# Attention followed by a gated feed-forward: reordered loads, and the mask-product scoring for the second half too

## The chip, the cores and the metric

The kernel runs on one core of one Trainium2 chip. The metric is the device time of one execution in microseconds; the time before is the median of six runs. A profile is one further execution with the hardware profiler on; its "span" runs from the first to the last recorded instruction.

## What is computed

Attention with 4 batches, 8 heads, 768 positions and head dimension 64, restricted to a window, and then a feed-forward with a relu gate. Cut to what matters:

```python
scores = scale * np.matmul(q, k.transpose(0, 1, 3, 2))
is_global = pos[None, :] < n_global                      # 8 global keys
is_local = (rel >= 0) & (rel < n_local)                  # the last 96 keys
keep = is_global | is_local
dist = np.where(is_global & ~is_local, n_local, np.abs(rel))
scores = np.where(keep, scores - slopes[h] * dist, -1e9) # a slope for each head
a = softmax(scores)
x = (a @ v) with heads joined                            # [3072, 512]
out = (np.maximum(x @ w_gate, 0) * (x @ w_val)) @ w_out  # 512 -> 1536 -> 512
```

Inputs and output are in float32; the kernel multiplies in bfloat16.

## The kernel before

The work is cut into eight *halves*, each half of the 768 positions of one batch (384 rows, all eight heads). Half 0 and half 1 belong to batch 0. A half goes through these steps, each a small function that is called from a hand-written order:

- `load_qk`, `load_v_half`: q and k come by SyncE's (SP) DMA queue into two staging buffers `qs`, `ks`; v comes by GpSimd's (POOL) queue, cast to bfloat16 on the way, into `vbuf`. The weights come by POOL's queue too, in three groups of four column blocks for the gate (`wg[0..2]`, `load_gate`) and for the value matrix (`wv[0..2]`, `load_val`), and as one piece for the output matrix (`wo_sb`).
- `piece_cast(s, p)`: casts q and k of head pair p to bfloat16.
- `piece_t(s, p)`: six TensorE transpositions into one PSUM bank, and copies from there into `qTb` and into the key tiles `kT` (`put_keys`).
- Scores, in one of two ways. For halves 0 and 1, `piece_bias` writes the distance bias into PSUM with a matmul (`sid` x `dd`), and `piece_score` adds q x k onto it, with one head in the upper and one in the lower 64 rows; an Exp on ScalarE (ACT) gives the weights `es`. The column groups of this way are in `first_groups`. For the later halves, `piece_qk` multiplies both heads of a pair at once, using a `qTb` in which each head's other 64 rows are zero; ACT takes the Exp, and VectorE (DVE) multiplies it with `m_all`, the exponentials of the bias, which `mask(h)` makes on ACT, one for each of the eight heads.
- Weights times v: `piece_av_wide` for halves 0 and 1 (a product with ones for the denominators, a product with v, then Ln, Exp and a multiplication into `xT`), `piece_av` for the later ones.
- `ffn_pieces(c)`: for each of twelve column blocks a gate product of four matmuls of 128x384 (relu on ACT, or on DVE for the blocks in `by_vector`) and a value product of four (multiplied by the relu on DVE into `ht`); and then six output pieces. In the list `f1`, item 2 fc is the gate product of block fc and item 2 fc + 1 is its value product.

From half 1 on the attention of the next half is woven between the feed-forward pieces of the one before. The order is written out by hand in every engine's program order (`manual_schedule`); `weave` places attention pieces at given fractions of the feed-forward work. The feed-forward has two PSUM banks in the stage around the change (`ffps2`), and `grelu` four buffers.

In the stage of the change POOL's program order is: value group 0 (behind a one-element copy that waits for half 0's `xT`), casts of half 1, v of half 1, gate group 1, a cast, fills of `kT` and `vbuf`, value group 1, fills of `qTb[0]`, gate group 2, fills of ones, value group 2. The q and k of half 1 are loaded from the middle of half 0's attention on (`load_qk_after(1, nc.vector, True)`, whose small memset stands on DVE and holds SP's DMAs back). PE's order is the first four gate products of half 0, half 1's attention with eight further products of half 0 in it, four more, then `other_pools()`; half 0's last eight products come in the second weave:

```python
    weave(f1_1[0 : 4 * GW],
          [(0.1 * h, lambda h=h: mask(h)) for h in range(H)],
          [(0.62 + 0.12 * p, lambda p=p: piece_t(2, p)) for p in range(HP)])
    weave(f1_0[G[2]] + f1_1[G[2]] + f2_0 + f2_1,
          spread(attention_pieces(2), 0.2, 0.9), ...
```

## Time and profile before

| | before |
|---|---|
| median of six runs | 254.24 us (252.97 to 256.0) |
| the profiled execution's own time | 254.06 us |
| its span | 252.3 us |
| TensorE busy | 241.5 us, 96% of the span |
| VectorE, ScalarE, GpSimd busy | 131.7, 157.5, 89.8 us |
| DMA | 33.15 MB in 77704 packets |
| granted TensorE clock | 1.00 |

The span and the execution's own time differ by 1.8 us, which lies around the recorded instructions. The page divides the span into 40 equal slices of 6.3 us; each digit is the busy share of an engine in tenths. "PE" is TensorE's matmuls, and their ends are modelled, so a busy PE is not a PE at its peak. The chain of waits is followed back from the last instruction: at each step to what released it, or to the instruction before it on the same engine. A group's row gives line, engine, operation, tiles and shapes, count, then total and mean time, then the engine's idle time just before and what ended it.

### The profile page before, as it was taken

How to read it: one execution, taken by the hardware profiler on the slowest of the kernel's cores; microseconds unless marked ns; L12 is line 12 of the kernel's file. 1: busy time of each engine (PE TensorE's matmuls, PEld its weight loads, DVE VectorE, ACT ScalarE, POOL GpSimd, SP SyncE). 2: the span in 40 equal slices, each digit the busy share in tenths (PEclk: the TensorE clock that was granted, in tenths of full speed). 3: DMA queues.
4: the chain of work that ended last, by engine and by line, in shares of the span. 5: the costliest groups of instructions: out<-in, count | busy, mean ns of one | idle time of the engine just before them, and what ended most of it. 6: DMA issues, size and time to landing. Idle time of an engine off the chain costs nothing.

```text
span 252.3 us, 4928 instructions
## 1 busy us (share of the span) xinstructions
PE 241.5 (96%) x1763; PEld 144.2 (57%) x1763; DVE 131.7 (52%) x338; ACT 157.5 (62%) x318; POOL 89.8 (36%) x214
## 2 busy tenths in 40 slices
PE   7788898999999999999999999999999999999994
PEld 3556565665555566556665566556565566556643
DVE  3635364695555557616662567617762557524410
ACT  5787555736676687657785687657785687553312
POOL 7818994600377426801537066302530000000000
PEclk9999999999999999999999999999999999999999
DMA  6999999980899983969376967729441200020012
GB/s 183 157 266 186 158 188 250 197 141 5 247 167 235 175 244 73 146 108 285 73 123 71 233 183 165 47 86 290 93 99 42 83 3 1 0 97 31 0 44 83
DMA packets 77704, 33.15 MB, mean 131 GB/s; under 512 B 53488, under 2 KB 74736, under 8 KB 77680
## 3 DMA queue, kind: packets, MB, share of 16 engines
q1 hardware_dynamic: 45824, 24.93, 36.3%
q0 software_dynamic: 31856, 7.91, 32.2%
q8 instruction: 14, 0.23, 0.4%
q14 instruction: 10, 0.08, 0.1%
...
## 4 chain that ended last, share of the span: by engine, by line
PE 80%; DMA 6%; DVE 5%; ACT 4%; SPq 2%; issue 1%; POOL 0%; ACTq 0%; DVEq 0%
PE ff_ps L521 24%; PE ff_ps L500 23%; PE ff_ps L487 21%; DMA qs<-in_q_dram 5%; PE av_ps L399 5%; PE qk_ps L371 4%; DVE xT L416 2%; SPq L131 2%; DVE ht L502 1%; ACT grelu L493 1%; PE av_ps L283 1%; ACT rcp L413 1%; ACT lnd L408 1%; DMA out_dram<-osb 1%; PE av_ps L433 1%
## 5 line engine op out<-in xcount | busy, mean ns | idle before, releaser
L500 PE MATMUL ff_ps<-xT,wv 128*128 128x384 bf16 x384 | 78.1, 326 | 1.5 <-ACT grelu L493 0.6
L487 PE MATMUL ff_ps<-xT,wg 128*128 128x384 bf16 x384 | 77.7, 326 | 0.3 <-DMA wg<-in_moe_w_gate_dram 0.3
L493 ACT ACTIVATE grelu<-ff_ps 128x384 bf16<-128x384 f32 x94 | 46.0, 490 | 32.7 <-PE ff_ps L487 18.4
L502 DVE TENSOR_TENSOR ht<-ff_ps,grelu 128x384 bf16<-128x384 f32 x96 | 53.2, 555 | 25.0 <-PE ff_ps L500 19.8
L521 PE MATMUL ff_ps<-wo_sb,ht 128*128 128x512 bf16 x276 | 64.5, 379 | 0.0
L416 DVE TENSOR_TENSOR xT<-av_ps,rcp 64x384 bf16<-64x384 f32 x48 | 26.6, 555 | 44.8 <-ACT rcp L413 44.1
L500 PEld LDWEIGHTS <-wv 128*128 128x128 bf16 x384 | 36.0, 97 | 24.5 <-issue 3.4
L487 PEld LDWEIGHTS <-wg 128*128 128x128 bf16 x384 | 36.1, 97 | 23.7 <-DMA wg<-in_moe_w_gate_dram 0.8
L383 DVE TENSOR_TENSOR es<-es,m_all 128x432 bf16<-128x432 bf16 (+5 forms) x108 | 33.2, 336 | 22.6 <-ACT es L374 22.1
L374 ACT ACTIVATE es<-qk_ps 128x432 bf16<-128x432 f32 (+2 forms) x72 | 37.9, 528 | 10.1 <-PE qk_ps L371 8.2
L521 PEld LDWEIGHTS <-ht 128*128 128x128 bf16 x276 | 25.8, 97 | 26.8
L296 POOL CAST kc<-ks 128x384 bf16<-128x384 f32 x20 | 9.7, 530 | 61.2 <-DMA ks<-in_k_dram 61.2
L408 ACT ACTIVATE lnd<-av_ps 64x384 f32<-64x384 f32 x48 | 23.3, 485 | 11.6 <-PE av_ps L399 11.0
L526 ACT COPY osb<-ff_ps 128x512 f32<-128x512 f32 x23 | 13.5, 586 | 23.3 <-PE ff_ps L521 22.5
L371 PE MATMUL qk_ps<-qT,kT 128*128 128x432 bf16 (+5 forms) x108 | 24.8, 286 | 0.0
L155 POOL DMA_DIRECT2D vbuf<-in_v_dram x28 | 24.4, 877 | 0.6 <-issue 0.6
L399 PEld LDWEIGHTS <-vbuf 128*128 128x128 bf16 x216 | 18.0, 98 | 7.4
L399 PE MATMUL av_ps<-es,vbuf 128*128 128x216 bf16 (+4 forms) x216 | 21.0, 226 | 0.0
L371 PEld LDWEIGHTS <-kT 128*128 128x128 bf16 x108 | 10.6, 98 | 7.6
L358 ACT ACTIVATE es<-qk_ps 128x864 bf16<-128x864 f32 (+3 forms) x16 | 10.5, 708 | 5.1 <-PE qk_ps L353 5.1
L304 POOL CAST qz<-qs 128x192 bf16<-128x192 f32 x40 | 12.7, 373 | 2.3 <-DMA qs<-in_q_dram 1.9
L413 ACT ACTIVATE rcp<-lnd 128x384 f32<-128x384 f32 x24 | 12.5, 522 | 0.8
...
## 6 DMA issues: line engine op xcount, KB each, us to landing
out_dram<-osb SPq DMA_DIRECT2D x23, 256.0 KB
...
```

What stands on the lines that cost most here:

```text
L155: nc.gpsimd.dma_start(out=v_dst(b, NG + r0, NG + r0 + n, j), in_=v[b, :, KT * j + r0 : KT * j + r0 + n, :].rearrange("h p d -> p h d"))
L371: nc.tensor.matmul(ps[:, c : c + n_], lhsT=kt[:, j, :], rhs=qd[:, :, :, a : a + w], start=True, stop=True)
L374: nc.scalar.activation(es[:, 0:cols], ps[:, 0:cols], AF.Exp, bias=0.0, scale=scale)
L383: nc.vector.tensor_mul(e4, e4, mk)
L399: nc.tensor.matmul(av3[:, :, a : a + w], lhsT=vb[:, j, z0 : z0 + 128], rhs=es[:, c : c + NN * w].rearrange("k (n p) -> k n p", n=NN), star ...
L408: nc.scalar.activation(ln[o0 : o0 + 64], av[d0 : d0 + 64, 0:QH], AF.Ln, bias=0.0, scale=1.0)
L416: nc.vector.tensor_tensor(xT_of[s][r, p, :], av_of[s, p, e_][r, 0:QH], rc[r], op=ALU.mult)
L487: nc.tensor.matmul(psg[:, 0:QH], lhsT=w_of(wg, dc, fc), rhs=xT[:, dc, :], start=(dc == 0), stop=(dc == N_DC - 1))
L493: nc.scalar.activation(gr, psg[:, 0:QH], AF.Relu, bias=0.0, scale=1.0)
L500: nc.tensor.matmul(psv[:, 0:QH], lhsT=w_of(wv, dc, fc), rhs=xT[:, dc, :], start=(dc == 0), stop=(dc == N_DC - 1))
L502: nc.vector.tensor_tensor(ht[:, fc, :], psv[:, 0:QH], st[fc], op=ALU.mult)
L521: nc.tensor.matmul(ps2, lhsT=ht[:, fc, n * 128 : (n + 1) * 128], rhs=wo_sb[:, fc, :], start=(fc == 0), stop=(fc == N_FC - 1))
```

## The change

Loads: the q and k of half 1 are no longer loaded during half 0's attention. Value group 0 is issued as soon as the fourth v piece of half 0 has landed, then gate group 1 behind gate group 0 and value group 1 behind value group 0, each held back by a one-element copy on POOL (`hold`) from the earlier landing's bytes. The q and k of half 1 follow behind gate group 1 (`load_qk_behind`), its v behind the first k, gate group 2 behind POOL's cast of pair 3, value group 2 behind half 1's first v piece, and half 2's q and k behind gate group 2.

Scoring: half 1 is scored by `piece_qk`, so its bias matmuls go and its mask products come; `mask` runs for all heads on ACT directly behind the first four gate products, instead of in the first weave. The two head rows of `qTb[1]` are copied separately, on ACT, and POOL zeroes the other rows. Casts of half 1 stand on ACT (pair 0), DVE (1 and 2) and POOL (3).

Order: all 24 gate and value products of half 0 now come before or inside half 1's attention, so the second weave has eight items less and its fractions are set anew. Four warm-up matmuls behind half 0's attention go. The pool of `es` has four buffers instead of three, and in the stage of half 1 the score pool has four banks in four tiles instead of two tiles of two banks.

```diff
--- before.py
+++ after.py
@@ -60,8 +60,7 @@
     by = {(h_, j): (j, a, w, m) for h_, j, a, w, m in spans}
     banks_of_half[0] = [[by[0, 0]], [by[0, 1]], [by[0, 2], by[0, 3]]]
     banks_of_half[1] = [[by[1, 2], by[1, 5]], [by[1, 3], by[1, 6]], [by[1, 4]]]
-    first_groups = [[[by[0, 0], by[0, 1]], [by[0, 2], by[0, 3]]],
-                    [[by[1, 4], by[1, 3]], [by[1, 5], by[1, 2], by[1, 6]]]]
+    first_groups = [[[by[0, 0], by[0, 1]], [by[0, 2], by[0, 3]]]]
 
     const = ctx.enter_context(tc.tile_pool(name="const", bufs=1))
     setupp = ctx.enter_context(tc.tile_pool(name="setupp", bufs=1))
@@ -77,19 +76,19 @@
     P = {}
     first = ExitStack()
     second = ExitStack()
-    P["es"] = second.enter_context(tc.tile_pool(name="es2", bufs=4))
+    P["es"] = first.enter_context(tc.tile_pool(name="es2", bufs=4))
     P["qk"] = first.enter_context(tc.tile_pool(name="qkps2", bufs=3, space=bass.MemoryType.PSUM))
 
     def second_pools():
         first.close()
-        P["qk"] = second.enter_context(tc.tile_pool(name="qkps3", bufs=2, space=bass.MemoryType.PSUM,
+        P["es"] = ctx.enter_context(tc.tile_pool(name="es", bufs=4, reuse_waits="tile"))
+        P["qk"] = second.enter_context(tc.tile_pool(name="qkps3", bufs=4, space=bass.MemoryType.PSUM,
                                                     reuse_waits="tile"))
         P["ff"] = second.enter_context(tc.tile_pool(name="ffps2", bufs=2, space=bass.MemoryType.PSUM,
                                                     reuse_waits="tile"))
 
     def other_pools():
         second.close()
-        P["es"] = ctx.enter_context(tc.tile_pool(name="es", bufs=3, reuse_waits="tile"))
         P["qk"] = ctx.enter_context(tc.tile_pool(name="qkps", bufs=3, space=bass.MemoryType.PSUM,
                                                  reuse_waits="tile"))
         P["ff"] = ctx.enter_context(tc.tile_pool(name="ffps", bufs=3, space=bass.MemoryType.PSUM,
@@ -177,15 +176,26 @@
     def load_val(i):
         load_w(wv[i], moe_w_val, i * GW * 128, (i + 1) * GW * 128)
 
-    def load_qk_after(s, eng, by_pairs=False):
+    def hold(dst, src):
+
+        nc.gpsimd.tensor_copy(dst, src)
+
+    def load_qk_behind(s, src):
 
         qs_of[s] = stage.tile([128, H, NN * D], FP32, name="qs")
         ks_of[s] = stage.tile([128, H, NN * D], FP32, name="ks")
-        step = 2 if by_pairs else H
+        for t in (ks_of[s], qs_of[s]):
+            hold(t[0:1, 0:H:2, 0:1], src[0:1, 0, 0:HP].unsqueeze(2))
+        for p in range(HP):
+            load_qk(s, 2 * p, 2 * p + 2)
+
+    def load_qk_after(s, eng):
+
+        qs_of[s] = stage.tile([128, H, NN * D], FP32, name="qs")
+        ks_of[s] = stage.tile([128, H, NN * D], FP32, name="ks")
         for t in (qs_of[s], ks_of[s]):
-            eng.memset(t[0:1, 0:H:step, 0:1], 0.0)
-        for h in range(0, H, step):
-            load_qk(s, h, h + step)
+            eng.memset(t[0:1, 0:1, 0:1], 0.0)
+        load_qk(s, 0, H)
 
 
     for p in range(HP):
@@ -247,8 +257,8 @@
             copy = nc.gpsimd.tensor_copy
             if s == 0:
                 copy = (nc.vector.tensor_copy, nc.scalar.copy, nc.scalar.copy, nc.vector.tensor_copy)[p]
-            elif s == 1 and p == 1:
-                copy = nc.scalar.copy
+            elif s == 1 and p < 3:
+                copy = (nc.scalar.copy, nc.vector.tensor_copy, nc.vector.tensor_copy)[p]
             copy(
                 qk[:, i].rearrange("t n e d -> t e n d"),
                 src[:, 2 * p : 2 * p + 2, :].rearrange("t e (n d) -> t e n d", n=NN))
@@ -284,12 +294,12 @@
                                  lhsT=qk[:, i, n],
                                  rhs=ident, is_transpose=True,
                                  start=(i == 0 and n == 0), stop=(i == 1 and n == NN - 1))
-        if s < 2:
+        if s == 0:
             nc.vector.tensor_copy(qTb[s][:, p, 0, :], tp[:, 0, :])
         else:
             for e in range(2):
                 r = slice(64 * e, 64 * e + 64)
-                nc.vector.tensor_copy(qTb[s % 2][r, p, e, :], tp[r, 0, :])
+                (nc.scalar.copy if s == 1 else nc.vector.tensor_copy)(qTb[s % 2][r, p, e, :], tp[r, 0, :])
         put_keys(nc.vector.tensor_copy, nc.vector.tensor_copy, kt, tp[:, 1, :], half)
 
     def piece_cast_k(s, p):
@@ -418,8 +428,10 @@
 
     def piece_av_wide(s, p):
 
-        todo = [t for group in first_groups[s] for t in group]
-        if p % 2 == 1:
+        todo = [t for group in (first_groups[0], banks_of_half[1])[s] for t in group]
+        if p % 2 == 1 and s == 1:
+            av = [P["qk"].tile([128, 512], FP32, name="qk_ps") for _ in range(2)]
+        elif p % 2 == 1:
             t = P["qk"].tile([128, 2, 512], FP32, name="qk_ps")
             av = [t[:, i] for i in range(2)]
         else:
@@ -430,9 +442,10 @@
                 es, c = es_of[s, p, j]
                 for e in range(2):
                     z0 = D + 2 * D * (2 * p + e)
+                    x = es[:, e, c : c + NN * w] if s == 0 else es[:, c + e * NN * w : c + (e + 1) * NN * w]
                     nc.tensor.matmul(av3[64 * e : 64 * e + 64, :, a : a + w],
                                      lhsT=ones if what == 0 else vbuf[0][:, j, z0 : z0 + D],
-                                     rhs=es[:, e, c : c + NN * w].rearrange("k (n p) -> k n p", n=NN),
+                                     rhs=x.rearrange("k (n p) -> k n p", n=NN),
                                      start=(i == 0), stop=(i == len(todo) - 1),
                                      skip_group_check=True)
         ln = rc_pool.tile([128, QH], FP32, name="lnd")
@@ -455,17 +468,15 @@
             return (C(0) + X(lambda: load_v_globals(0), lambda: load_v(0, 0), lambda: load_v(0, 1),
                              lambda: load_v(0, 2), lambda: load_v(0, 3), lambda: load_gate(0))
                     + C(1) + T(0) + BI(0, 0, 1) + C(2) + T(1) + SC(0, 0, 1) + BI(1, 0) + SC(1, 0) + C(3) + T(2)
-                    + BI(1, 1) + SC(1, 1) + BI(2, 0) + T(3) + X(lambda: copy_v_globals(0, 1, 4), lambda: load_qk_after(1, nc.vector, True))
+                    + BI(1, 1) + SC(1, 1) + BI(2, 0) + T(3) + X(lambda: copy_v_globals(0, 1, 4))
                     + SC(2, 0) + BI(2, 1) + SC(2, 1)
                     + BI(3, 0) + SC(3, 0) + BI(3, 1) + SC(3, 1)
                     + AW(0) + AW(1) + AW(2)
-                    + AW(3) + X(second_pools, lambda: warm(4)))
+                    + AW(3) + X(second_pools))
         if s == 1:
             f = [[x] for x in fill]
-            return (T(0) + BI(0, 0, 1) + T(1) + SC(0, 0, 1) + T(2) + BI(1, 0) + SC(1, 0) + BI(1, 1) + SC(1, 1)
-                    + T(3) + BI(2, 0) + SC(2, 0) + BI(2, 1) + SC(2, 1) + f[0] + BI(3, 0) + SC(3, 0)
-                    + f[1] + BI(3, 1) + SC(3, 1) + f[2] + AW(0) + f[3] + AW(1) + f[4]
-                    + AW(2) + f[5] + f[6] + AW(3) + f[7])
+            return (f[0] + C(0) + C(1) + T(0) + C(2) + T(1) + f[1] + QK(0) + T(2) + QK(1) + T(3) + f[2] + QK(2) + f[3] + QK(3)
+                    + AW(0) + AW(1) + f[4] + AW(2) + f[5] + AW(3) + f[6] + f[7])
         AV = lambda p: [(0.29, lambda e=e: piece_av(s, p, e)) for e in range(2)]
         g = QK(3)
         a = AV(2)
@@ -562,44 +573,50 @@
     copy_v_globals(0, 4, NT)
     for p in range(HP):
         nc.gpsimd.memset(kT[0][p][:, 6, NG + 48 : 128].bitcast(mybir.dt.uint32), 0)
-
-    nc.gpsimd.tensor_copy(wv[0][0:1, 0, 0:1], xT_of[0][0:1, 0, 0:1])
+    hold(wv[0][32:33, 0, 0:1], v_dst(0, 32, 33, 3)[:, 0, 0:1])
     load_val(0)
-    piece_cast(1, 0)
-    load_v_half(1)
-    piece_cast(1, 2)
+    for e in range(2):
+        nc.gpsimd.memset(qTb[1][64 - 64 * e : 128 - 64 * e, :, e, :].bitcast(mybir.dt.uint32), 0)
+    hold(wg[1][0:1, 0, 0:1], wg[0][0:1, 0, 0:1])
     load_gate(1)
-    piece_cast(1, 3)
+    hold(wv[1][0:1, 0, 0:1], wv[0][0:1, 0, 0:1])
+    load_val(1)
+    load_qk_behind(1, wg[1])
     for p in range(HP):
         nc.gpsimd.memset(kT[1][p][:, 3, 32:128].bitcast(mybir.dt.uint32), 0)
         nc.gpsimd.memset(kT[1][p][:, 6, NG + 48 : 128].bitcast(mybir.dt.uint32), 0)
     nc.gpsimd.memset(vbuf[1][:, NT - 1, :].bitcast(mybir.dt.uint32), 0)
-    load_val(1)
+    hold(v_dst(0, 32, 33, 4)[:, 0, 0:1], ks_of[1][32:33, 0, 0:1])
+    load_v_half(1)
+    piece_cast(1, 3)
+    load_gate(2)
     for e in range(2):
         nc.gpsimd.memset(qTb[0][64 - 64 * e : 128 - 64 * e, :, e, :].bitcast(mybir.dt.uint32), 0)
-    load_gate(2)
+    hold(wv[2][32:33, 0, 0:1], v_dst(0, 32, 33, 4)[:, 0, 0:1])
+    load_val(2)
+    load_qk_behind(2, wg[2])
     for j in range(NT):
         fill_ones(nc.gpsimd, 1, j)
-    load_val(2)
-    load_qk_after(2, nc.gpsimd, True)
-
-    f1_0, f2_0 = ffn_pieces(0, range(GW, 2 * GW - 2))
+
+    f1_0, f2_0 = ffn_pieces(0, (5, 7, 8))
     f1_1, f2_1 = ffn_pieces(1)
     G = [slice(2 * GW * i, 2 * GW * (i + 1)) for i in range(N_FC // GW)]
-    for i in (0, 2):
+    for i in (0, 2, 4, 6):
         f1_0[i][1]()
-    piece_cast(1, 1)
-    for i in (4, 6):
+    for h in range(H):
+        mask(h)
+    for i in (1, 3, 5, 7, 8, 10, 12, 14):
         f1_0[i][1]()
-    for _, f in attention_pieces(1, [f1_0[i] for i in (1, 3, 5, 7, 8, 10, 9, 11)]):
+    for _, f in attention_pieces(1, [f1_0[i] for i in (9, 11, 13, 15, 16, 18, 20, 22)]):
         f()
-    for i in (12, 13, 14, 15):
+    for i in (17, 19, 21, 23):
         f1_0[i][1]()
     other_pools()
     load_v_globals(1)
     load_v_half(2)
+    piece_cast(2, 0)
     load_w(wo_sb, moe_w_out, 0, DM)
-    for p in range(HP):
+    for p in range(1, HP):
         piece_cast(2, p)
     spread_v_globals(1)
     for i in range(2):
@@ -607,13 +624,12 @@
     e3 = early_pieces(3)
     ck, xk, cq, xq, od = e3[0:HP], e3[HP : HP + NN], e3[HP + NN : 2 * HP + NN], e3[2 * HP + NN : -HP], e3[-HP:]
     weave(f1_1[0 : 4 * GW],
-          [(0.1 * h, lambda h=h: mask(h)) for h in range(H)],
-          [(0.62 + 0.12 * p, lambda p=p: piece_t(2, p)) for p in range(HP)])
-    weave(f1_0[G[2]] + f1_1[G[2]] + f2_0 + f2_1,
-          spread(attention_pieces(2), 0.2, 0.9), [(0.25, lambda: load_qk_after(3, nc.vector))],
-          spread(ck + cq, 0.4, 0.45), [(0.45, lambda: load_v_half(3))],
-          spread(xk, 0.52, 0.56), spread(xq, 0.64, 0.68), spread(od, 0.93, 0.97),
-          [(0.55 + 0.05 * j, lambda j=j: fill_ones(nc.vector, 0, j)) for j in range(NT)])
+          [(0.62 + 0.1 * p, lambda p=p: piece_t(2, p)) for p in range(HP)])
+    weave(f1_1[G[2]] + f2_0 + f2_1, [(0.05, lambda: load_qk_after(3, nc.vector))],
+          spread(attention_pieces(2), 0.02, 0.88),
+          spread(ck + cq, 0.25, 0.31), [(0.31, lambda: load_v_half(3))],
+          spread(xk, 0.4, 0.45), spread(xq, 0.55, 0.6), spread(od, 0.91, 0.96),
+          [(0.44 + 0.06 * j, lambda j=j: fill_ones(nc.vector, 0, j)) for j in range(NT)])
 
     for c in range(2, NHALF):
         placed = []
```

## The prediction

> **What bounds the kernel now.** I read the page first, for where TensorE is not full:
>
> ```profile
> span 252.3 us, 4928 instructions
> ...
> PE   7788898999999999999999999999999999999994
> ...
> ACT  5787555736676687657785687657785687553312
> POOL 7818994600377426801537066302530000000000
> PEclk9999999999999999999999999999999999999999
> DMA  6999999980899983969376967729441200020012
> ```
>
> Each digit is a slice of 6.3 us. TensorE (PE) is at nine tenths or more from about 45 us to the end; the holes lie in the first seven slices, while the DMA row is high and the granted clock never leaves 9. So time can be won or lost only before about 45 us, unless a later stage gets a new hole. Next, busy time by stretch:
>
> ```profile
> core 0: us, PE busy (x) PEld busy (x) DVE busy (x) ACT busy (x) POOL busy (x), PEclk, DMA share, GB/s
> 0.00:18.20 18.20, 14.15 (x164) 8.76 (x164) 8.65 (x34) 13.38 (x29) 10.84 (x26) 1.00 1.10 196
> 18.20:41.60 23.40, 21.05 (x249) 13.82 (x250) 11.62 (x31) 13.28 (x24) 19.05 (x41) 1.00 1.26 194
> 41.60:46.80 5.20, 5.20 (x34) 3.13 (x32) 2.23 (x4) 3.78 (x9) 2.67 (x6) 1.00 1.69 216
> ```
>
> The first column of pairs is the stretch and its length, then each engine's busy time and instruction count. From 18.2 us (first gate product) to 41.6 us TensorE is busy 21.05 of 23.40 us, and matmul ends are modelled, so the holes are rather larger. ScalarE (ACT) and VectorE (DVE) have 10 and 12 us free. Then the chain of waits, in order of time (start, length, what):
>
> ```profile
> 16.53 9.04 DMA qs<-in_q_dram
> 25.57 0.05 issue
> 25.62 0.52 POOL qk L252
> 26.14 0.05 issue
> 26.19 0.51 PE av_ps L283 x6
> ...
> 38.73 0.50 ACT grelu L493
> ```
>
> The second half's last q lands at 25.57 us, GpSimd casts it, TensorE transposes it at 26.19: TensorE waited 1.3 us there. The line at 38.73 is a relu between two products on the two PSUM banks. The rows that price the steps:
>
> ```profile
> L493 ACT ACTIVATE grelu<-ff_ps 128x384 bf16<-128x384 f32 x94 | 46.0, 490 | 32.7 <-PE ff_ps L487 18.4 <-DVE ht L502 11.6
> L374 ACT ACTIVATE es<-qk_ps 128x432 bf16<-128x432 f32 x36 | 19.0, 528 | 5.7 <-PE qk_ps L371 4.6
> L374 ACT ACTIVATE es<-qk_ps 128x480 bf16<-128x480 f32 x24 | 13.6, 567 | 1.7 <-PE qk_ps L371 1.1
> L234 ACT ACTIVATE m_all<-dd 128x432 bf16<-128x432 bf16 x8 | 4.2, 554 | 0.0
> ```
>
> (mean ns stands behind the total), and for a weight group, issue to landing, least, median, most:
>
> ```profile
> DMA to landing us min/median/max: 5.5/8.1/9.0
> ```
>
> **A common mark.** Both kernels at some moment have done the same TensorE work: the 24 gate and value products of half 0 and half 1's whole attention. Call it M; what follows is the same work, TensorE-bound in both. Before, 16 of the 24 are done at 41.61 us in the chain; the other eight come later at 0.65 us each (4 x 384 columns), so M = 41.61 + 8 x 0.65 = 46.8 us. The change in time is the change in M.
>
> **TensorE's part.** Chain pieces: a product 0.65, or 0.76 next to a 64-wide product (0.76 at 29.32 to 38.05); a transposition 0.34; one head pair's three score groups by the later halves' way 0.20 + 0.20 + 0.18 = 0.58; one by bias and score 0.35 + 0.26 + 0.28 + 0.23 = 1.12; one wide value step 0.74. After: 24 x 0.65 + 4 x 0.34 + 4 x 0.58 + 4 x 0.74 + 4 x 0.11 = 22.7 us. The first product still waits for the last xT (VectorE, 18.09 + 0.56 = 18.65), some 0.3 us, so M cannot come before 18.2 + 22.7 + 0.3 = 41.2. Before, the same sum is 22.7 + 4 x 0.54 + 0.3 = 25.2 and ends at 43.4: 3.4 us were waits. Removing the bias products is 2.2 us, the waits are 3.4: 5.6 us at most. The four warm-up products that go lie in a gap that ends with xT, so they give nothing. The gap behind half 0's value steps is then at most 18.65 - 16.9 = 1.8 us; the clock stayed at 1.00 over the 1.3 us hole at 24.9, so I price it at nothing. [...]
>
> **ScalarE's part, which I think decides.** Its queue from its first relu (19.06 us) to the last gate's, in order: 9 relus of the 12 (three go to VectorE) at 0.49 = 4.4; 8 mask exponentials at 0.55 = 4.4, formerly under half 1's products where ScalarE had idle time; one pair's two casts 1.0; 8 copies of 64 x 384 for qT, formerly VectorE's (0.35 there; no row on ScalarE: between 0.35 and the 0.51 of its 128 x 384 cast; I take 0.485, its Ln on 64 x 384) = 3.9; 12 score exponentials 4 x (0.567 + 0.567 + 0.528) = 6.6; 4 Ln and Exp pairs 4 x (0.49 + 0.52) = 4.0. Sum 24.3 us. Neighbours overlap: two relus took 0.87 instead of 0.98, two masks 1.00 instead of 1.11, so some 0.1 each over about 40, and 20.3 are left. ScalarE must wait besides: 0.8 while TensorE paces the first relus, 1.0 before each of the relus of gates 4 and 6 together (their products queue for two banks behind the masks), 0.7 for the first transposition, 0.1 in each Ln-Exp pair, 0.8 before the last Ln and relu: 3.7 us. So the relu of gate 10 is done near 19.06 + 20.3 + 3.7 - 0.4 = 42.7 (one relu less than the list), and the last four value products follow, 4 x 0.65: M = 45.3, with a hand-over 45.4. With no overlap at all the sum is 4.0 longer, M = 49.4; with the small waits hidden too, M = 44.4. I take 45.4, because the overlap is in the rows and the waits are likewise.
>
> **VectorE's part.** It loses 4 qT copies (1.4) and gains 20 mask products (per pair 0.48 + 0.48 + 0.37 in the rows at 84.7 to 91 us: 5.3), four casts (0.36 to 0.41 each, 1.5) and one relu more. From about 27 us on its list is 1.5 + 2.7 keys + 5.3 + 4 x 0.5 + 2 x 0.5 + 4 x 0.5 = 14.5 us, ending near 42, just under ScalarE: it is next late if ScalarE is quicker, and hides nothing more. POOL's casts of pair 3 run beside these products: POOL's casts took 0.50 to 0.66 with such products about, so I add 0 to 0.3. [...]
>
> **The loads.** POOL issues each weight group behind a one-element copy that waits for an earlier landing. Fourth v: issue 8.85 + 4.6 = 13.4, then value group 0: issue 13.6 + 5.5 = 19.1, needed at 21.0. Gate group 1 waits for gate group 0 (9.76 + 6.5 = 16.3): lands 22.1, needed 23.9. Value group 1 waits for value group 0: 19.3 + 5.5 = 24.8, needed 27. The second q and k wait for gate group 1; SP then issues eight at 0.47: first pair down 2.7 us after the first issue, as at the start (0.74 to 3.42), so 25.2, cast wanted at 26.9; last pair 4.5 after its issue (4.32 to 8.86), 30.5. Nothing else stands behind these on SP. On POOL, behind the wait for the second k, stand its v, then the cast of pair 3 (two at 0.51), done near 31.6, wanted by the fourth transposition near 31.7, then gate group 2: 32 + 5.5 = 37.5, wanted at 38.0. Value group 2 comes behind two fills of 0.75: 34.3 + 5.5 = 39.8, wanted at 42.7. Half 2's q and k wait for gate group 2: first pair down at 40.5, wanted by the first weave's transpositions at 52. All in time, the cast of pair 3 and gate group 2 with half a microsecond or less. The moved output weights: 19.4 us from issue near 46 would be 65.4 against about 65 for first use; the queue ahead is shorter than before, so nothing. The second weave has the same pieces per product as before (0.83 and 0.81 us), so no new hole.
>
> **The sum.** M from 46.8 to 45.4 is -1.4 us. The profiled execution took 254.06 us (span 252.3 and 1.8 around it), 0.18 under the median of six, 254.24: 252.66 for it, 252.8 us for the median. About 0.5%, 1.27 us, is what a measurement of this kernel can tell from no change.
>
> **The rivals.**
> (1) Slower: the loads come late and POOL's order turns it into a stall. Place: gate group 2 is issued only behind the cast of pair 3. In the trace the second q took 9.04 us from its last issue (16.53 to 25.57) beside GpSimd's queue traffic; so here 26 + 9 = 35, cast done 36, gate group 2 down at 42, 4 us after gate 8 wants it. TensorE then has 8 products, two value steps and small waits left, 7.5 us: M = 49.5, +2.7, 256.9 us. It decides from a cast later than about 32 us; at 33 it cancels most of the gain. For it: the margin and that lagging row; against it: the row's transfer began while gate group 0 was still in flight, here only v and value group 1 are.
> (2) Faster: ScalarE's operations overlap or wait less and TensorE bounds the stage: M = 41.2 + 1.3 for the hand-overs that remain = 42.5, -4.3, some 250. Against it: two engines with over 20 us of ordered work in 23.
> (3) No change: overlap fails for a third of the operations, M near 46.8, 254.2.
>
> **Chances.** Forecast 0.52, own range 251.6 to 254.0; of it 0.32 is past -0.5%, 0.20 within. Rival 1: 0.28 (0.25 slower, 0.03 within). Rival 2: 0.15, all faster. Rival 3: 0.05, within. Faster 0.47, same 0.28, slower 0.25. The range leaves out the outer part of rivals 1 and 2: 250.4 to 256.9.
>
> **What would show it.** Right: no bias matmuls after 18 us, products from 18.2 to 27 us without a hole over 0.6, masks on ScalarE from about 21.5 to 25.3, ScalarE over 90% busy from 28 to 41, gate 10's relu near 42.7, TensorE full from then on, clock 1.00 throughout. Wrong: TensorE waiting for a weight landing or a cast of the second half (rival 1), ScalarE with gaps of a microsecond while TensorE is full (rival 2), or a hole after 50 us at the output weights or half 2's transpositions.

## The result, and the profile after

The changed kernel takes 255.66 us (median of 31 executions, 254.15 to 257.82); the kernel before, on the same chip, 254.00 us (68 executions). The ratio is 1.0083, 95% interval 1.0064 to 1.0102: slower by 0.8%, where the prediction's likeliest case was 0.6% faster. The profiled execution took 257.15 us, 1.5 us over its median, with a span of 255.4 us.

The page after, in the same slices as before (6.4 us each):

```profile
span 255.4 us, 4848 instructions
...
PE   6768798999999999999999999999999999999994
...
ACT  5788489334576677747875677647775677643312
POOL 7742567940183707620645146400640000000000
PEclk9999979999999999999999999999999999999999
DMA  6998999992759994696462987928451200021012
```

From the eighth slice on TensorE is as full as before. The third and fifth slices have *more* holes than before (6 and 7 tenths where both had 8), although the change was to fill them, and the clock row, which had only nines, has a 7 in the sixth. The same stretches as in the prediction, each with its length, then every engine's busy time and instruction count, and TensorE's granted clock in the third column from the end:

```profile
0.00:18.20 18.20, 12.36 (x159) 7.85 (x159) 8.95 (x32) 13.38 (x29) 12.29 (x28) 1.00 1.05 158
18.20:41.60 23.40, 19.54 (x151) 11.41 (x152) 14.36 (x46) 17.26 (x37) 11.88 (x34) 0.93 1.10 181
41.60:46.80 5.20, 4.79 (x60) 2.83 (x58) 3.17 (x8) 4.76 (x10) 5.20 (x9) 1.00 1.03 272
```

Between 18.2 and 41.6 us TensorE was to lose its waits; it is busy 19.54 us instead of 21.05, at a mean clock of 0.93. The granted clock stood at one half for one window of 3.41 us (second row; the first row is the window before it):

```profile
28.10:31.50 3.40, 1.50 (x14) 0.82 (x14) 2.06 (x5) 1.97 (x4) 2.48 (x4) 1.00 1.01 299
31.50:34.91 3.41, 3.41 (x22) 2.23 (x20) 2.72 (x12) 2.12 (x5) 1.98 (x5) 0.50 1.69 179
```

The chain of waits has three loads where it had one (start, length, what):

```profile
9.77 8.57 DMA wg<-in_moe_w_gate_dram
...
18.87 6.32 DMA wg<-in_moe_w_gate_dram
...
26.90 3.91 DMA qs<-in_q_dram
...
31.32 0.70 PE av_ps L293 x6
32.02 1.28 PE ff_ps L511 x4
...
33.74 1.46 ACT es L384 x3
...
36.09 1.46 ACT es L384 x3
...
41.39 0.77 DVE es L393 x3
```

Gate group 0, then gate group 1 behind it, then the second half's q behind that. The timeline of TensorE shows what each wait did; the bracket holds the idle time ahead of a row and what ended it:

```profile
18.39 2.86 PE L498 MATMUL ff_ps<-xT,wg 128*128 128x384 bf16 x16 [1.48 <-DMA wg<-in_moe_w_gate_dram]
22.08 2.99 PE L511 MATMUL ff_ps<-xT,wv 128*128 128x384 bf16 x16 [0.82 <-DMA wv<-in_moe_w_val_dram]
25.33 2.92 PE L498 MATMUL ff_ps<-xT,wg 128*128 128x384 bf16 x16 [0.26 <-DMA wg<-in_moe_w_gate_dram]
...
29.74 0.51 PE L293 MATMUL av_ps<-ident,qk 128*128 128x128 bf16 x6 [0.82 <-ACT qk L262]
31.32 0.70 PE L293 MATMUL av_ps<-ident,qk 128*128 128x128 bf16 x6 [1.07 <-DVE qk L262]
```

Gate group 0 made TensorE wait (it lands at 18.34), value group 0, gate group 1, and then the casts of the first and second pair of half 1's q and k. The mark M of the prediction (24 gate and value products and half 1's attention done) comes at 48.9 us, from 46.65 in the trace of before: +2.2 us, where -1.4 was expected. Behind 50 us TensorE is idle 0.6 us more in all than before; two of the new holes are 0.26 us at 63.0 and 0.38 at 76.7, in the second weave. (These two are counted between the starts of matmuls, since their ends are modelled; the brackets of a timeline count from the modelled ends and show some 0.16 us less. The holes of e9 and e15 below are counted in the same way.) Two and a quarter at M, 0.2 between M and 50 us and 0.6 behind it are the 3.1 us between the two spans. The medians differ by 1.7 only: the profiled execution is one of those with a half-rate window. By granted clock, 17 of 32 executions of the changed kernel had no such window (mean 255.4 us) and 15 had one or more (256.2). The kernel before had one in 50 of the 144 executions made beside the experiments; in each group of them those without took 253.8 to 254.0 us on average, those with one 255.6 to 256.2. Without windows the change costs some 1.5 us.

### The profile page after: what moved, and what is told of

It is laid out like the page before. It is cut to its first block, busy times and chain, and to the rows that moved or that the text cites. A ratio compares the mean times of both kernels' runs of the same rounds, so it can differ in the third digit from the quotient of the medians.

```text
span 255.4 us, 4848 instructions
## 1 busy us (share of the span) xinstructions
PE 240.4 (94%) x1699; PEld 141.8 (56%) x1699; DVE 137.5 (54%) x357; ACT 160.8 (63%) x329; POOL 90.4 (35%) x218
## 4 chain that ended last, share of the span: by engine, by line
PE 71%; DVE 8%; DMA 8%; ACT 6%; POOL 3%; issue 2%; SPq 0%; POOLq 0%; ACTq 0%; DVEq 0%
PE ff_ps L532 23%; PE ff_ps L511 20%; PE ff_ps L498 18%; DMA wg<-in_moe_w_gate_dram 6%; PE av_ps L409 5%; PE qk_ps L381 4%; DVE ht L513 3%; DVE xT L426 2%; DMA qs<-in_q_dram 2%; POOL vbuf L154 1%; ACT rcp L423 1%; ACT lnd L418 1%; ACT es L384 1%; DVE es L393 1%; ACT grelu L504 1%
## 5 line engine op out<-in xcount | busy, mean ns | idle before, releaser
L513 DVE TENSOR_TENSOR ht<-ff_ps,grelu 128x384 bf16<-128x384 f32 x96 | 53.2, 555 | 24.9 <-PE ff_ps L511 20.9
L426 DVE TENSOR_TENSOR xT<-av_ps,rcp 64x384 bf16<-64x384 f32 x48 | 26.7, 555 | 45.7 <-ACT rcp L423 44.9
L384 ACT ACTIVATE es<-qk_ps 128x432 bf16<-128x432 f32 (+2 forms) x84 | 43.5, 533 | 11.8 <-PE qk_ps L381 10.0
L393 DVE TENSOR_TENSOR es<-es,m_all 128x432 bf16<-128x432 bf16 (+6 forms) x128 | 38.2, 332 | 21.2 <-ACT es L384 20.5
L532 PEld LDWEIGHTS <-ht 128*128 128x128 bf16 x276 | 25.7, 97 | 26.4
L381 PE MATMUL qk_ps<-qT,kT 128*128 128x432 bf16 (+6 forms) x128 | 29.0, 292 | 0.6 <-ACT qT L302 0.3
L409 PEld LDWEIGHTS <-vbuf 128*128 128x128 bf16 x216 | 18.2, 98 | 8.2 <-issue 0.5
L381 PEld LDWEIGHTS <-kT 128*128 128x128 bf16 x128 | 12.7, 100 | 9.6 <-DVE kT L281 0.9
L293 PE MATMUL av_ps<-ident,qk 128*128 128x128 bf16 x72 | 6.5, 232 | 2.8 <-ACT qk L262 1.6
```

Of the source, the lines that this page charges most:

```text
L381: nc.tensor.matmul(ps[:, c : c + n_], lhsT=kt[:, j, :], rhs=qd[:, :, :, a : a + w], start=True, stop=True)
L384: nc.scalar.activation(es[:, 0:cols], ps[:, 0:cols], AF.Exp, bias=0.0, scale=scale)
L393: nc.vector.tensor_mul(e4, e4, mk)
L409: nc.tensor.matmul(av3[:, :, a : a + w], lhsT=vb[:, j, z0 : z0 + 128], rhs=es[:, c : c + NN * w].rearrange("k (n p) -> k n p", n=NN), star ...
L426: nc.vector.tensor_tensor(xT_of[s][r, p, :], av_of[s, p, e_][r, 0:QH], rc[r], op=ALU.mult)
L513: nc.vector.tensor_tensor(ht[:, fc, :], psv[:, 0:QH], st[fc], op=ALU.mult)
```

## Experiments

All are compared in up to five rounds with the kernel before on the same chip. "Span" and "M" are those of one profiled execution each, "windows" is the number of executions whose mean granted clock was 0.9955 or less: the profiled execution of the changed kernel, with one half-rate window of 3.41 us, has 0.993.

| kernel | ratio to before (95%) | median | span | M | windows |
|---|---|---|---|---|---|
| changed kernel | 1.0083 (1.0064, 1.0102) | 255.66 | 255.4 | 48.9 | 15 of 32 |
| e1, no holds between weight groups | 1.0035 (1.0002, 1.0068) | 255.18 | 253.8 | 47.1 | 5 of 12 |
| e2, matmuls of zeros in the holes | 1.0110 (1.0052, 1.0167) | 256.83 | 253.9 | 47.2 | 2 of 6 |
| e3, loads and order without the scoring | 1.0049 (1.0013, 1.0084) | 255.53 | 252.3 | 46.1 | 1 of 12 |
| e4, scoring without loads and order | 1.0172 (1.0124, 1.0221) | 258.71 | 257.2 | - | 6 of 6 |
| e5, no second q and k | 1.0075 (1.0038, 1.0113) | 255.85 | 254.6 | 48.1 | 7 of 12 |
| e6, half the qT copies off ScalarE | 1.0097 (1.0064, 1.0131) | 256.17 | 253.8 | 47.5 | 3 of 12 |
| e7, all of them off, scores by two banks | 1.0082 (1.0047, 1.0118) | 256.19 | 255.2 | 48.4 | 5 of 12 |
| e8, e7 without the holds | 1.0047 (1.0010, 1.0083) | 255.44 | 251.8 | 45.4 | 4 of 12 |
| e18, e3 without the holds | 1.0028 (0.9996, 1.0060) | 255.24 | 253.6 | 47.2 | 1 of 12 |
| e9, second weave alone | 1.0091 (1.0048, 1.0134) | 257.22 | 255.1 | - | 8 of 12 |
| e15, e8 with the eight products put back | 1.0187 (1.0139, 1.0235) | 258.44 | 256.2 | - | 2 of 6 |
| e10, before with mask products | 1.0046 (1.0011, 1.0080) | 255.78 | 252.2 | 46.1 | 12 of 12 |
| e14, e10 with matmuls of zeros | 0.9994 (0.9970, 1.0018) | 254.11 | 252.4 | 47.0 | 2 of 12 |
| e11, before with a cast and a product moved | 0.9964 (0.9930, 0.9998) | 253.57 | 252.8 | 47.4 | 4 of 12 |
| e12, e10 and e11 together | 0.9987 (0.9951, 1.0022) | 254.50 | 252.1 | 44.9 | 9 of 12 |
| e13, e12 with three output buffers | 0.9982 (0.9937, 1.0027) | 253.47 | 250.7 | 44.8 | 8 of 12 |
| e16, e13 with four masks earlier | 0.9967 (0.9935, 0.9999) | 253.58 | 251.6 | 45.8 | 6 of 12 |
| e17, e16 with matmuls of zeros | 0.9955 (0.9919, 0.9991) | 253.12 | 251.7 | 45.7 | 0 of 12 |

M varies by a microsecond or so with the landings of one execution (the first gate product alone starts between 16.8 us, in e3, and 18.6, in e14), so it places a loss and the ratio sizes it.

### The serial hand-offs: e1

```diff
-    hold(wg[1][0:1, 0, 0:1], wg[0][0:1, 0, 0:1])
     load_gate(1)
-    hold(wv[1][0:1, 0, 0:1], wv[0][0:1, 0, 0:1])
     load_val(1)
```

> The changed kernel without the two one-element copies that hold gate group 1 behind gate group 0 and value group 1 behind value group 0; the second half's q and k still wait for gate group 1. Theory A (the hand-offs between loads cost the time): gate group 1 lands at about 22.5 us instead of 25.2 and the first q and k pair at about 25.5 instead of 28.6; the holes before the first value product (about 1 us), the second gate group (0.4), and the first two transpositions (1.0 and 1.2) shrink below 0.5 each, the half-clock stretch at 31 to 34 us goes with them, and the kernel is 2.5 to 3.5 us faster than the changed one, that is 0.3 to 1.5 us faster than the kernel before. Rival B (ScalarE's and VectorE's list for half 1's attention sets the end of the stage): the loads come earlier, but the last relu of half 0 is done no more than 0.7 us earlier and the time stays 1 to 2 us above the kernel before.

1.0083 becomes 1.0035: by the ratios about 1.2 us, more than half of the loss, was two one-element copies. The size is uncertain: the two intervals overlap by 0.0004, and among executions without a half-rate window the means are 255.4 (17) and 255.1 us (7). The 2.5 to 3.5 us of theory A did not come: in e1's trace gate group 1 no longer makes TensorE wait, but the first value product still waits 1.06 us for value group 0, and the second transposition 1.18 us for a cast. GpSimd's own rows in the changed kernel show what a link costs:

```profile
14.22 0.76 POOL L171 DMA_DIRECT2D wv<-in_moe_w_val_dram  x1 [0.30 <-POOL wv L181]
...
18.40 0.18 POOL L181 COPY wg<-wg 1x1 bf16<-1x1 bf16 x1 [1.89 <-DMA wg<-in_moe_w_gate_dram]
18.87 0.74 POOL L171 DMA_DIRECT2D wg<-in_moe_w_gate_dram  x1 [0.30 <-POOL wg L181]
...
22.00 0.18 POOL L181 COPY wv<-wv 1x1 bf16<-1x1 bf16 x1 [2.39 <-DMA wv<-in_moe_w_val_dram]
22.49 0.74 POOL L171 DMA_DIRECT2D wv<-in_moe_w_val_dram  x1 [0.31 <-POOL wv L181]
```

The copy wakes when the last of the load's 16 shares is down (gate group 0's at 18.34 us, the copy at 18.40). Then come 0.5 us to the issue, the issue itself and the way of the first bytes, 2.0 us from an issue's start to its first packet in the packet records (18.87 to 20.87 us for gate group 1): 2.5 us in which this queue brings nothing of the next group. One link is more than the 1.8 us that the prediction left between the landing of gate group 1 and its need. Without the two holds the three groups are issued back to back in e8, which lacks the fills of `qTb[1]` too, and the q and k are released at 22.8 us instead of 25.3. In e1, where these fills stand between (1.5 us), that is at 24.5. e8:

```profile
14.01 0.76 POOL L172 DMA_DIRECT2D wv<-in_moe_w_val_dram  x1 [0.30 <-POOL wv L182]
14.75 0.75 POOL L172 DMA_DIRECT2D wg<-in_moe_w_gate_dram  x1
15.49 0.76 POOL L172 DMA_DIRECT2D wv<-in_moe_w_val_dram  x1
22.82 0.18 POOL L182 CAST ks<-wg 1x4 f32<-1x4 bf16 x1 [6.58 <-DMA wg<-in_moe_w_gate_dram]
```

### The clock, first try: e2

```diff
+        if s == 1 and p < 2:
+            for _ in range(4):
+                nc.tensor.matmul(tp, lhsT=wo_sb[:, 0, 0:128], rhs=wo_sb[:, 0, :], start=True, stop=True)
```

These stand ahead of half 1's first two transpositions.

> The changed kernel with four matmuls of 128x512 on zeros ahead of each of the first two transpositions of half 1, where TensorE stood idle for 1.0 and 1.2 us. Theory C (the granted clock, 0.5 for about 3 us after those holes, costs by itself): the clock stays at 1.00 in that stage, the matmuls between 31 and 34 us run at full rate, and the time falls by 1.0 to 1.6 us against the changed kernel. Theory B: those matmuls had slack beside ScalarE and VectorE, so 0 to 0.4 us. If the fillers outlast the waits, up to 0.8 us is lost.

No gain (1.0110, six executions), and two of the six had a window all the same. In these places the holes are as long as the loads are late, so eight fixed matmuls may neither fill them nor be free; this is argued, not shown. e2 did not settle the clock's part; e14 says more.

### The two parts of the change by themselves: e3, e18, e4

e3 is the kernel before with the new loads, holds, casts and order of products, but with bias and score matmuls in half 1; e18 is e3 without the two holds. e4 is the changed kernel with the old loads and order, and the eight masks behind the first four gate products.

```diff
 e3:  load_qk_behind, hold and the casts of the change; second weave of the change
-            return (f[0] + C(0) + C(1) + T(0) + C(2) + T(1) + f[1] + QK(0) + T(2) + QK(1) + ...
+            return (f[0] + C(0) + C(1) + T(0) + BI(0, 0, 1) + C(2) + T(1) + f[1] + SC(0, 0, 1) + T(2) + ...
 e4:  load_qk_after(1, nc.vector, True) in half 0, POOL's order and both weaves of before
+            return (T(0) + T(1) + QK(0) + T(2) + QK(1) + f[0] + T(3) + QK(2) + f[1] + QK(3)
```

> The kernel before with the new order of loads, of products and of casts alone: half 1 is still scored with bias matmuls and without mask products, and the mask exponentials stay in the first weave. Theory A: all of the loss comes with the loads, so this is 1 to 4 us slower than the kernel before, with the same holes before the first value product and the first transpositions. Rival B: the loads by themselves fill TensorE's holes, and it is 1 to 2 us faster than before.

> e3 (the change's loads, order and casts on bias scoring, ratio 1.0049) without the two holds between weight groups. With the holds it lost 0.5%; the holds were worth 0.5% in the changed kernel (1.0083 to 1.0035) and 0.35% in its two-bank form (1.0082 to 1.0047). If chain and scoring add up, the ratio is 1.000 to 1.002. If the order of the products costs by itself (casts of half 1's q and k then stand late, between 27 and 31 us, whatever the holds), it stays at 1.003 to 1.005.

> The changed kernel's scoring of half 1 alone: loads, casts, the order of the feed-forward products and the warm-up matmuls as in the kernel before; mask exponentials behind the first four gate products, qT copies on ScalarE. Theory A: the scoring takes 2.2 us of bias products off TensorE and puts 5.3 us on VectorE and 3.7 + 3.9 us on ScalarE, which have room there: 0.5 to 2 us faster than before. Rival B: the longer chain of score, Exp, mask product and value step takes back what the bias products gave: 0 to 2.5 us slower than before.

With the new loads the time is 1.0049 with holds and bias products, 1.0028 without holds, 1.0083 with holds and mask products, 1.0035 with masks and no holds. So removing 2.2 us of bias products (0.9%) gained nothing in either pair, the holds cost 0.2% on the bias form, within the noise, and the new order lost about 0.3% even with no hold in it (its interval just reaches 1). e4 is a miss of its own: it priced a bad place for the masks, not the scoring.

```profile
22.15 3.73 ACT L233 ACTIVATE m_all<-dd 128x432 bf16<-128x432 bf16 x8
25.77 1.94 ACT L291 COPY qT<-av_ps 64x384 bf16<-64x384 bf16 x4
```

The eight masks stand ahead of the qT copies on ScalarE, the scores wait for the copies, and TensorE stood still for 4.6 us (from 22.2), followed by two half-rate windows (granted clock 0.50 from 24.98 us).

### Is it the second q and k, or ScalarE's list? e5, e6, e7, e8

```diff
 e5
-    load_qk_behind(1, wg[1])
+    qs_of[1], ks_of[1] = qs_of[0], ks_of[0]
 e6
-                (nc.scalar.copy if s == 1 else nc.vector.tensor_copy)(qTb[s % 2][r, p, e, :], tp[r, 0, :])
+                (nc.scalar.copy if s == 1 and e == 0 else nc.vector.tensor_copy)(qTb[s % 2][r, p, e, :], tp[r, 0, :])
 e7, in piece_score, with one dense qT copy on VectorE as before
+                nc.vector.tensor_mul(e4, e4, m_all[:, 2 * p : 2 * p + 2, 0 if j == 0 else 1, :, m : m + w])
 e8: e7 without the two holds
```

e5 computes half 1 from half 0's q and k. e7 keeps each head in its own 64 rows and its own PSUM bank, so ScalarE loses all eight qT copies (3.8 us) while the mask products stay.

> The changed kernel with half 1's attention fed from half 0's staged q and k, so that the second q and k are never loaded and never waited for (half 1's output is not the reference's); weights, v and all else as in the changed kernel. Theory A (the second q and k come too late): the holes before the first two transpositions (1.0 and 1.2 us) go, and so does the half-clock stretch behind them; 1.5 to 2.5 us faster than the changed kernel. Theory B (ScalarE's list for half 1's attention is the bound from its first score Exp on): the list starts about 2 us earlier too, but gives back to VectorE and to the PSUM banks; no more than 0.5 us faster.

> The changed kernel with one of the two q copies of each of half 1's transpositions on VectorE instead of ScalarE: ScalarE's list is 4 x 0.48 = 1.9 us shorter, VectorE's 4 x 0.36 = 1.4 us longer, and the two run beside each other, so that the keys' copies follow sooner. Theory B: ScalarE was full from 33.7 to 41.2 us (12 Exps of 5.7 us and four q copies of 1.9 us in the profile), so the last Exp comes 1 to 1.9 us earlier and the time falls by 0.7 to 1.5 us. Theory A: 0 to 0.3 us.

> Half 1 scored with mask products, but from the kernel before's layout: each head in its 64 rows and its own PSUM bank, no bias matmuls, q copied once per pair by VectorE (0.36 us) instead of twice by ScalarE (0.96); two Exps per pair (0.85 + 0.65) instead of three (1.66). The new order of loads, products and casts is kept. Theory B: ScalarE's list is 3.9 + 0.6 us shorter, VectorE's 1.4 us longer: 1.5 to 2.5 us faster than the changed kernel. Theory A alone: 0 to 0.7 us, as the transpositions come no sooner.

> The last one without the two one-element copies between weight groups 0 and 1. If both theories hold, their gains add: 2 to 4 us faster than the changed kernel, that is 0.3 to 2 us faster than the kernel before. If the loads alone count, it is no faster than the changed kernel without the chain (1.0035 of the kernel before).

Without any transfer of the second q and k the kernel is no faster (1.0075): gate group 1 was still late, with gate product 4 at 26.4 us. Taking 1.9 or 3.8 us off ScalarE changed nothing either (1.0097, 1.0082), until the holds went too (e8, 1.0047), and then no more than in e1. ScalarE's list, which the prediction took for the bound, is not what decides here: it begins with the casts of q and k, and these wait for loads, in the changed kernel for the second k (28.60 us), in e5 behind the relus of the products that wait for gate group 1 (29.02 us).

### The second weave: e9 and e15

```diff
 e9, on the kernel before
-    for i in (12, 13, 14, 15):
+    for i in range(12, 24):
         f1_0[i][1]()
-    weave(f1_0[G[2]] + f1_1[G[2]] + f2_0 + f2_1, ...
+    weave(f1_1[G[2]] + f2_0 + f2_1, ...
 e15, on e8
-    for _, f in attention_pieces(1, [f1_0[i] for i in (9, 11, 13, 15, 16, 18, 20, 22)]):
+    for _, f in attention_pieces(1, [f1_0[i] for i in (9, 11, 13, 15)]):
-    weave(f1_1[G[2]] + f2_0 + f2_1, ...
+    weave(f1_0[G[2]] + f1_1[G[2]] + f2_0 + f2_1, ...
```

> The kernel before, with one part of the change alone: half 0's last eight gate and value products run ahead of the first weave, and the second weave has the change's fractions; loads and scoring are those of before. Theory W (part of the loss lies in the second weave, where eight products fewer are left to cover half 2's attention): TensorE idles 3.5 to 3.9 us after 50 us where before idles 3.0, with the two holes that after shows at 63.0 and 76.7 us (0.26 and 0.38), and the time is 0.5 to 0.8 us above before, a ratio of 1.002 to 1.003. Rival (the later holes are a follow-on of the late first stage): idle after 50 us stays at 3.0 and the ratio within 0.001 of 1.

> The best form of the changed kernel so far (e8: no chain of holds, two-bank scores; ratio 1.0047), with half 0's last eight products and the second weave's fractions put back as before has them; half 1's attention is then covered by four products fewer at its end. Theory W (the second weave, with 5.2 us less to cover half 2's attention, costs 0.6 us after 50 us): idle after 50 us falls by 0.5 to 0.8 us to before's 3.0, and the two holes near 60 and 73 us go; against it stand 0.5 to 1.5 us more of holes in half 1's attention. Expected ratio 1.003 to 1.008; M cannot be compared here, the end of the trace can.

e9 was slower by as much as the whole change, but not for the reason under test. In its trace TensorE idles as long behind 50 us as before does (nine further gaps of 0.21 us, exactly one 128x512 matmul each, are taken as records missing from the trace). The time is lost at 42 to 49 us, where moved products run pair by pair through the two PSUM banks of that stage with five gaps of 0.23 us between gate and value, and at 22.5 us, where a cast was 2.4 us late in that execution, with a half-rate window behind it; 8 of its 12 executions had a window, and the four others took 255.0 us on average. One of the two later holes is there all the same: 0.38 us at 77.0 us, where a value step waits for xT as in the changed kernel, and before has none. It comes with the second weave; two holes of 0.17 us that before has (96.5 and 148.1 us) are gone in its place. The other, of 0.26 us, stands near 59 to 63 us in every kernel here with the change's loads and order (e1, e3, e5 to e8, e18) and not in e9; what makes it stays open. e15 goes the other way: with four products fewer as cover, half 1's attention waits 1.5 and 1.9 us at 33 and 39 us, and the kernel is 1.9% slower, where 0.3 to 0.8% was expected. These four are needed where the change put them, given that order (of its 24 products, four others stand directly behind that attention).

### Mask products where their price can be seen: e10, e14

The kernel before, with its loads and order, and two masks made just ahead of each pair's exponentials.

```diff
+            M = lambda p: X(lambda: mask(2 * p), lambda: mask(2 * p + 1))
-            return (T(0) + BI(0, 0, 1) + T(1) + SC(0, 0, 1) + T(2) + BI(1, 0) + SC(1, 0) + BI(1, 1) + SC(1, 1) + ...
+            return (T(0) + T(1) + M(0) + SC(0, 0, 1) + T(2) + M(1) + SC(1, 0) + SC(1, 1) + ...
 e14
+            X(lambda: warm(2)) ahead of SC(0, 0, 1), X(lambda: warm(2)) ahead of SC(1, 0), X(lambda: warm(6)) ahead of T(3)
```

> The kernel before, with the second half's bias matmuls replaced by mask products on VectorE, each head in its own rows and bank as before, and each pair's two masks made on ScalarE just before that pair's exponentials (before's trace leaves ScalarE 0.4 to 1.5 us idle at each of those places). Loads, order and fill are those of before. Theory S (TensorE's sum decides in that stage): 2.2 us less of bias products, M falls from 46.7 to 44.5 to 45.5, the ratio is 0.991 to 0.996. Rival (the bias products only fill time in which TensorE waits for casts and loads of the q and k pairs): M within 0.5 us of before, ratio 0.998 to 1.003.

> The kernel with mask products alone (e10), with ten matmuls of zeros (0.21 us each) in the holes that the removed bias products leave (two ahead of the first scores, two ahead of the second pair's, six ahead of the last transposition). Theory C (e10 loses by the clock: all its 12 runs had a half-rate window, 13 of 35 of before): fewer than half of the runs have such a window, and the ratio falls from 1.0046 to 0.996 to 1.000. Rival (ScalarE, full from 19.0 to 31.3 us in e10 with its eight masks, sets the stage's end whatever the clock): windows may go, but the ratio stays at 1.002 to 1.006.

Taking 2.2 us of matmuls off TensorE made the kernel 0.46% slower, and every one of its 12 executions had a half-rate window. In the profiled one the window before the drop was

```profile
22.09:25.50 3.41, 1.63 (x26) 1.15 (x26) 3.14 (x15) 3.41 (x8) 1.71 (x4) 1.00 1.79 173
```

TensorE busy 1.63 of 3.41 us, where the kernel before had 2.28 in its emptiest window of that stretch. e14 puts ten matmuls of zeros, 2.1 us of pure waste, into the places of the bias products: windows fall from 12 of 12 to 2 of 12 and the ratio from 1.0046 to 0.9994; the two intervals overlap by less than 0.1%. ScalarE's list is the same in both. The bias products were standing in waits for casts and for the last q; without them the waits remain, and the clock drops. No execution of e10 was without a window, so what it would take at full rate is not shown; e14's ten without one took 253.9 us on average, as before's did, so ten matmuls of zeros were as free in these places as the bias products.

### What does shorten the stage: e11, e12, e13, e16, e17

```diff
 e11, on the kernel before: cast of half 1's pair 2 from POOL to ScalarE, behind the first gate products
-            elif s == 1 and p == 1:
+            elif s == 1 and p in (1, 2):
-    load_v_half(1)
-    piece_cast(1, 2)
+    load_v_half(1)
 and a value product ahead of the last transposition
-                    + T(3) + BI(2, 0) + ...
+                    + f[0] + T(3) + BI(2, 0) + ...
 e12: e10's and e11's edits, f[0] + f[1] ahead of T(3)
 e13: e12 with
+        P["osb"] = ctx.enter_context(tc.tile_pool(name="osb", bufs=3))
 e16: e13 with mask(0), mask(1) in half 0 behind its second pair's scores, mask(2), mask(3) ahead of gate 0
 e17: e16 with warm(2) ahead of SC(0, 0, 1) and warm(2) ahead of SC(1, 0)
```

> The kernel before, with two things moved: the cast of half 1's third q and k pair from GpSimd, where it stands behind a 2.5 us issue of V, to ScalarE, and the first value product ahead of the last transposition. Before's trace has holes of 0.57 and 1.13 us there (idle ended by a GpSimd cast). If these holes lie on the path that sets the end, the first is gone and 0.65 us of the second is covered: 0.8 to 1.2 us, ratio 0.995 to 0.997. If ScalarE's exponentials set the stage's end, the holes move to later places and the ratio is 0.999 to 1.003.

> The edits of the two kernels before this one together, with two value products ahead of the last transposition. If TensorE's sum and the cast holes both count, M falls by 2 to 3 us and the ratio is 0.988 to 0.993, faster than both kernels. If the bias products only filled waiting time, it is no better than the kernel with moved casts alone (0.995 to 1.000).

> The kernel with moved casts and mask products (e12), with three buffers for output tiles in place of two. In e12's trace ScalarE's copies of output tiles wait 3.07 and 1.01 us for output stores near 80 us, the last attention's reciprocal lies behind them, and half 2's first gate product waits 1.08 us for xT, so that its fourth matmul starts at 83.91, where before's starts at 83.94 although before's first stage ended 1.7 us later. Theory G (the gain is given back there): the wait goes, the time falls by 0.8 to 1.2 us, ratio 0.993 to 0.996. Rival (the output tiles wait for the DMA anyway, a third buffer only moves the wait): ratio 0.998 to 1.000.

> e13 with the first two masks made in half 0, where ScalarE is idle for 1.34 us at 10.5 us, and the next two ahead of half 0's first gate products, where it is idle for 1.0 us. ScalarE's full stretch in half 1 loses 2.0 us. If ScalarE's list bounds that stage once the bias products are gone, the time falls by a further 0.5 to 1.5 us against e13, ratio 0.988 to 0.994. If not (casts and the arrival of the last q pair set it), it is within 0.2% of e13.

> e16 (ratio 0.9967; 6 of 12 runs with a half-rate window) with four matmuls of zeros in its holes at 21.2 and 22.6 us, two ahead of each. Its runs at full clock had a mean of 253.08 us, those with a window 254.1. If the fill keeps the clock, windows fall to 2 or 3 of 12 and the mean to 253.2 to 253.5 (ratio 0.994 to 0.997). If the fill delays the scores by its own 0.85 us, the ratio is 0.998 to 1.001.

e11 touches only the two holes that the trace of before shows at 22.6 and 24.9 us, and is faster than both kernels, by little: 0.9964, with an interval up to 0.9998. Its profiled execution does not show the gain: the third q came late there, the cast on ScalarE waited 1.78 us for it, and M is 47.4. e12 reached M 1.7 us earlier than before, 0.9 of it already at the first gate product (17.24 for 18.19 us), and gained nothing clear, where 0.7 to 1.2% was expected; its trace shows where the gain went. Four lines, of ScalarE in e12, of TensorE in e12, and of ScalarE in the kernel before:

```profile
80.52 0.59 ACT L533 COPY osb<-ff_ps 128x512 f32<-128x512 f32 x1 [3.07 <-DMA out_dram<-osb]
```

```profile
83.91 0.32 PE L494 MATMUL ff_ps<-xT,wg 128*128 128x384 bf16 x1 [1.08 <-DVE xT L422]
```

```profile
80.51 0.59 ACT L526 COPY osb<-ff_ps 128x512 f32<-128x512 f32 x1 [1.80 <-PE ff_ps L521]
81.12 0.99 ACT L408 ACTIVATE lnd<-av_ps 64x384 f32<-64x384 f32 x2
```

Both copies of an output tile start at 80.5 us: before, because TensorE's products are done; in e12, because one of two output buffers is still being stored, beside the loads of v. Half 2's last Ln and Exp queue behind that copy, and half 2's first gate product waits for xT. With a third buffer (e13) the wait is gone from ScalarE's list, and the span falls to 250.7 us, 1.6 under before. Its four executions without a window took 252.8 us on average, but 8 of 12 had one, so its ratio is only 0.9982, where 0.993 to 0.996 was expected. Masks out of ScalarE's full stretch (e16) did not keep the clock: 6 of 12 had a window, and 0.9967 is e13's ratio within the noise. With four matmuls of zeros besides (e17) there was no window in 12 executions: 253.12 us, 0.9955 (0.9919, 0.9991), the fastest median here and 2.5 us under the changed kernel. Against executions of before without a window, e17 gains 0.5 us; about half of its 1.1 us goes with the windows.

## Why the prediction was wrong

**The step that failed is the term of the loads.** "Fourth v: issue 8.85 + 4.6 = 13.4, then value group 0: issue 13.6 + 5.5 = 19.1": the 5.5 is the least of the three landing times in the row that it came from, 5.5/8.1/9.0, taken for a transfer that shares the queue with gate group 0. It measured 14.22 to 21.95, 7.7 us: thirteen of its sixteen shares were down at 19.8, and the last came 2.2 us behind them. "Gate group 0 (9.76 + 6.5 = 16.3)" landed at 18.34, because the last of its shares came late (fifteen of sixteen were down at 17.61), and the trace of before had shown such a landing. Two lines of it, the landings of the three gate groups (least, median, most) and TensorE's first product:

```profile
DMA to landing us min/median/max: 6.5/6.8/8.4
18.19 2.87 PE L487 MATMUL ff_ps<-xT,wg 128*128 128x384 bf16 x16 [0.32 <-DMA wg<-in_moe_w_gate_dram]
```

The 6.5 is again the least. Gate group 0, issued at the same 9.76 us, is the 8.4: it was down at 18.14, and TensorE's first product waited for it. So the first link of the chain, taken to start at 16.3, could have been known to start at 18.1. Gate group 1 came at 25.20 instead of 22.1, the first q and k cast could start at 28.60 instead of 26.9, pair 3 was cast at 34.1 instead of 31.6. "All in time" should have been: late by 1 to 3 us, each load starting from the one before. The mechanism is that of rival 1, loads that come late, in another place. Its named place, gate group 2 behind the cast of pair 3, didn't decide: the group landed at 39.57 (a transfer of 5.5 us, with little beside it), and gate product 8 asked for it at 41.13, since everything ahead of it was late too. The cast was past the 33 us from which the rival was to cancel most of the gain.

**ScalarE's operations were sized well, but ScalarE did not decide.** The rows:

```profile
L384 ACT ACTIVATE es<-qk_ps 128x432 bf16<-128x432 f32 x40 | 21.1, 529 | 6.5 <-PE qk_ps L381 5.6
L384 ACT ACTIVATE es<-qk_ps 128x480 bf16<-128x480 f32 x32 | 17.8, 569 | 2.5 <-PE qk_ps L381 1.8
L302 ACT COPY qT<-av_ps 64x384 bf16<-64x384 bf16 x8 | 3.8, 473 | 1.5 <-PE av_ps L293 1.4
L244 ACT ACTIVATE m_all<-dd 128x432 bf16<-128x432 bf16 x8 | 3.7, 551 | 0.0
```

The copy onto ScalarE, taken at 0.485 us between 0.35 and 0.51, is 0.473; exponentials and masks are as priced. But the list could only begin with the casts: ScalarE was busy 78% of the time from 28 to 41 us, not over 90%, and gate 10's relu was done at 46.1 us, not near 42.7. e6 and e7 took 1.9 and 3.8 us out of the list and gained nothing, so it was not the bound in this order.

**TensorE's part.** "Removing the bias products is 2.2 us" counts work that stood in waits. e10, e14 and the pairs e18 to e1 and e3 to the changed kernel show no gain from it. A sum of busy time per engine, here 21.05 of 23.40 us, doesn't tell which busy time is cover.

**The clock, priced at nothing.** The prediction took it that the clock would stay at 1.00 behind a single hole, as it had in the trace of before. The drop to 0.50 followed a window in which TensorE was busy for 1.50 of 3.40 us, cut up by holes of 0.99 and 1.23 us between starts (0.82 and 1.07 in the brackets above); none was longer than before's 1.13 us (bracket at 26.19 us), whose window had TensorE busy for 2.28 of 3.41 us and was followed by a clock of 1.00. So the longest hole did not tell the two kernels apart here; the busy time of the window did. As for the price: between executions with and without a window it is 0.8 us in the changed kernel (256.2 and 255.4) and some 2 us in the kernel before (255.6 to 256.2, and 253.8 to 254.0). An execution with a window may also be one in which something came late, so neither difference need be the clock alone.

**GpSimd beside VectorE's products.** The casts of pair 3 took 0.50 and 0.51 us and ended at 34.10, before the first mask product at 34.34, so the two casts did not try the price of 0 to 0.3 us. Smaller ones did meet mask products: casts of four elements took 0.31 and 0.32 us in the changed kernel and a one-element copy 0.64 in e8, against 0.18 elsewhere.

**The second weave, "no new hole"**, was wrong by 0.6 us in the changed kernel; 0.38 of it is the hole that e9 has too, and the rest is open. The output weights, issued at 47.28, delayed nothing. The wide range of 250.4 to 256.9 us held the result, by rival 1's end of it; the forecast's own, 251.6 to 254.0, did not.

Together: of the 2.1 us that the ratio stands for (1.7 between the medians), 0.5 to 1.2 is the chain of holds (three pairs: e3 to e18, e7 to e8, the changed kernel to e1; only the last is clear of the noise). About 0.7 is the new order itself (e18, at the edge of what these runs resolve); that late casts and thin cover make it is argued from the traces, not tested apart. The bias products' 2.2 us bring nothing against it. How much is paid through the clock is not shown: windows came in 15 of 32 executions of the changed kernel, 5 of 12 of e1, and 1 of 12 of e3 and of e18.
